# A transformer block on one core: all weights from float64 by two Prelu steps and one shift-or, the last additions on VectorE, the order computed anew

## The chip, the cores and the metric

The kernel runs on one core of a Trainium2 chip. The core's engines work side by side, each on a queue of its own: TensorE (PE; the loading of weights is shown apart, as PEld), VectorE (DVE), ScalarE (ACT), GpSimd (POOL) and SyncE (SP), which issues transfers. They wait for each other by semaphores. The metric is device microseconds of one execution. TensorE's clock has two levels, 1.2 and 2.4 GHz; the profile shows the granted clock as a share of the higher one.

## The reference

Softcapped attention, then a mixer over tokens and over channels, then the real part of a two-dimensional FFT with a normalisation and a second channel mixer. Batch 4, 12 heads, 448 tokens, 768 channels; cap is 30.

```python
scores = cap * np.tanh(scale * np.matmul(q, k.transpose(0, 1, 3, 2)) / cap)
attn = np.exp(scores - max); attn = attn / (sum + 1e-09)
x = attn @ v                                     # (4, 448, 768)
u = x + (np.maximum(x^T @ w_tok1, 0) @ w_tok2)^T   # 448 -> 256 -> 448
x = u + np.maximum(u @ w_ch1, 0) @ w_ch2           # 768 -> 1536 -> 768
u = x + np.real(fft2(x))
un = (u - mean) / np.sqrt(var + 1e-06)
out = u + np.maximum(un @ m_ch1, 0) @ m_ch2        # 768 -> 3072 -> 768
```

(Shortened: `max`, `sum`, `mean` and `var` are over the last axis.) The six weight matrices come as float64.

## The kernel before

**Storage.** Activations lie as 128 channels by 896 columns (two batches of 448 tokens): `z[bp][kc]`, bp 0 or 1 for the pair of batches, kc 0 to 5 for the block of channels; in traces `z_75` to `z_86`. Every product is made in three matmuls of rounded numbers (`mm3`, lines 248 to 250): a weight and an activation are each split into a high part and a low rest, and high·high, high·low and low·high are added up in PSUM. A weight of 128x768 with its parts is a *piece* (tiles `wh`, `wl`, four slots); PSUM has four slots `mm`, of 128 by two halves of 448.

**Weights from float64.** The chip's engines compute in float32, so a float64 weight is made from its two 32-bit words, or from bytes. There are two ways in the kernel before:
- `convert_v` (line 291), for the two pieces of each token-mixer matrix and the first two pieces of `c1`: ScalarE squares the high word, VectorE makes the bits with a shift-and (L313) and two and-or, shift-or steps (L317, L320), and a comparison and product (L323) clears tiny numbers.
- `convert` (line 331), for the other 70: the transfer (L351) lies three bytes off, so that the first word has the low bits of the exponent and the mantissa; three Relu steps on ScalarE (L276) make two powers of two out of the top byte, `cva` and `cvf`; on VectorE a shift-or (L359) makes the mantissa, an addition of integers (L279) joins the two powers, and one product (L368) makes the number.
- Then both split it: `wh` on ScalarE (L276), `wl` on VectorE or GpSimd (L279).

All elementwise sums of two tensors are recorded by one helper (L279) and all ScalarE copies by another (L276), so the tiles' names tell them apart.

**Order.** A planner (`Plan`) sorts all operations before they are emitted. It has for each a list of engines that it may take with an estimate of its time (`v`: VectorE; `a`: ScalarE; `t`: TensorE; `vp`: VectorE or GpSimd, whichever would end first), a rank from the order in which the program records it plus a shift by key (`SHIFT`), and constants (`fixed`) for what each instruction costs above its length. Each engine then runs its own list in that order; a change anywhere can move operations everywhere.

**Stages**, with their place in the profile: attention heads and token mixer (0 to about 290 us); first channel mixer (`group`, to about 700); the spectrum, `transform`, for either bp (560 to 840), which ends by adding its result `r` to `z`; the second mixer in 12 *Halves* for bp = 0 (to about 1100), in which a piece of m1 or m2 is converted, multiplied, and summed into `z`; for these `hidden` (L788, L792) makes the ReLU and its high and low parts (`r`), and `down` multiplies by the second weight and adds to `z`. Out of the converted m pieces, kept as `u` in float32, `combine` makes sums and differences of four (`u<-u`), which go to DRAM (`kept`). With them the second mixer of bp = 1 runs as Strassen products (1060 to the end). Their last sums, in `fold_in`, `fold_out`, `last15`, `last67` and `last23`, gather the products into the `z` of bp = 1, of two `z` tiles (`z<-z`) or of PSUM and `z` (`z<-mm,z`), and `store` writes them out (L1167).

## Time and profile before

| | |
|---|---|
| time, three runs | 1403.98, 1405.87, 1405.85 us (median 1405.85) |
| the profiled execution | 1406.29 us; its span 1404.40 us |
| TensorE busy | 1365.7 us, 97% of the span, 7470 instructions |
| VectorE busy | 1073.5 us, 76% |
| ScalarE busy | 704.1 us, 50% |
| GpSimd busy | 321.5 us, 23% |
| TensorE's granted clock, mean | 0.994 |
| the chain that ended last | PE 70%, DVE 15%, ACT 6%, DMA 5% |

The times agree within 0.2%. The page gives busy time by engine, the span in slices, and groups of instructions; the trace behind it gives the same for a stretch (from : to, in us from the span's start), the waits of one engine by the instruction that ended them, and single instructions in order of time. A busy TensorE is not TensorE at full clock: the granted clock stands beside it. An engine that idles costs nothing unless TensorE waits for it.

### The profile page before, as it was taken

How to read it: one execution, taken by the hardware profiler on the slowest of the kernel's cores; microseconds unless marked ns; L12 is line 12 of the kernel's file. 1: busy time of each engine (PE TensorE's matmuls, PEld its weight loads, DVE VectorE, ACT ScalarE, POOL GpSimd, SP SyncE). 2: the span in 40 equal slices, each digit the busy share in tenths (PEclk: the TensorE clock that was granted, in tenths of full speed). 3: DMA queues.
4: the chain of work that ended last, by engine and by line, in shares of the span. 5: the costliest groups of instructions: out<-in, count | busy, mean ns of one | idle time of the engine just before them, and what ended most of it. 6: DMA issues, size and time to landing. Idle time of an engine off the chain costs nothing.

```text
span 1404.4 us, 18761 instructions
## 1 busy us (share of the span) xinstructions
PE 1365.7 (97%) x7470; PEld 1135.0 (81%) x7470; DVE 1073.5 (76%) x1153; ACT 704.1 (50%) x824; POOL 321.5 (23%) x169
## 2 busy tenths in 40 slices
PE   8899999999999999999998999999999999999996
PEld 3344444599999999899998989988989998999996
DVE  7999988566776756557889699888977646667688
ACT  7878887576555544123233235444544553543432
POOL 4342433100000001000001122432314404414354
PEclk9999999999999999999999999999999999999999
DMA  4223221015666566512231168787868433344452
GB/s 125 86 73 105 83 73 47 7 68 157 247 201 194 193 222 207 160 46 91 90 136 57 46 223 298 272 309 259 301 229 298 152 113 100 103 124 133 130 178 99
DMA packets 67353, 211.90 MB, mean 151 GB/s; under 512 B 7552, under 2 KB 8960, under 8 KB 67266
## 3 DMA queue, kind: packets, MB, share of 16 engines
q1 hardware_dynamic: 66112, 208.08, 44.4%
q0 software_dynamic: 1152, 2.62, 0.7%
q8 instruction: 59, 0.97, 0.3%
q14 instruction: 28, 0.23, 0.0%
q10 hardware_dynamic: 2, 0.00, 0.0%
HBM read 145.30 MB, written 65.37 MB: 150 GB/s over the span
## 4 chain that ended last, share of the span: by engine, by line
PE 70%; DVE 15%; ACT 6%; DMA 5%; issue 2%; POOL 1%; SPq 0%; DVEq 0%; ACTq 0%; POOLq 0%
PE mm L249 20%; PE mm L248 20%; PE mm L250 20%; DVE t L279 3%; PE av L579 3%; DVE m L279 2%; DMA raw<-in_m_dram 2%; DMA wl<-kept 2%; PE sc L511 2%; DVE z L279 2%; ACT t L536 2%; ACT t L516 2%; PE av L595 2%; DVE u L279 2%; PE mx L706 1%
## 5 line engine op out<-in xcount | busy, mean ns | idle before, releaser
L249 PE MATMUL mm<-u,wh 128*128 128x448 f32 x798 | 293.7, 368 | 0.2 <-DVE u L279 0.2
L248 PE MATMUL mm<-u,wh 128*128 128x448 f32 x774 | 284.9, 368 | 4.9 <-DVE z L279 3.3
L250 PE MATMUL mm<-u,wl 128*128 128x448 f32 x774 | 284.6, 368 | 2.3 <-DMA wl<-kept 2.3
L279 DVE TENSOR_TENSOR z<-mm,z 128x896 f32<-128x896 f32 (+1 forms) x210 | 214.0, 1031 | 62.8 <-PE mm L250 61.4
L248 PE MATMUL mm<-r,wh 128*128 128x448 f32 x696 | 255.7, 367 | 0.7 <-DVE r L279 0.3
L249 PE MATMUL mm<-r,wh 128*128 128x448 f32 x678 | 249.4, 368 | 6.9 <-DVE r L279 6.6
L250 PE MATMUL mm<-r,wl 128*128 128x448 f32 x696 | 254.9, 366 | 0.0
L249 PEld LDWEIGHTS mm<-u,wh 128*128 128x128 f32 x798 | 151.1, 189 | 13.0 <-DVE u L279 0.6
L248 PEld LDWEIGHTS mm<-u,wh 128*128 128x128 f32 x774 | 146.5, 189 | 18.1 <-issue 3.7
L250 PEld LDWEIGHTS mm<-u,wl 128*128 128x128 f32 x774 | 146.5, 189 | 15.3 <-DMA wl<-kept 2.7
L276 ACT ACTIVATE cva<-raw 128x768 bf16<-128x768 int8 x70 | 63.4, 906 | 172.0 <-DVE u L368 66.4
L249 PEld LDWEIGHTS mm<-r,wh 128*128 128x128 f32 x678 | 127.8, 188 | 19.7 <-DVE r L279 8.7
L248 PEld LDWEIGHTS mm<-r,wh 128*128 128x128 f32 x696 | 131.2, 188 | 13.0 <-ACT r L276 0.8
L250 PEld LDWEIGHTS mm<-r,wl 128*128 128x128 f32 x696 | 131.2, 188 | 10.9
L528 POOL PARTITION_ALL_REDUCE mb<-m x48 | 93.6, 1997 | 166.9 <-DVE m L279 151.0
L276 ACT ACTIVATE r<-mm 128x896 fp32r<-128x896 f32 (+5 forms) x81 | 66.6, 826 | 119.2 <-PE mm L250 54.6
L279 DVE TENSOR_TENSOR t<-t,mb 112x1792 f32<-112x1792 f32 x48 | 107.3, 2254 | 5.5 <-POOL mb L528 5.4
L516 ACT ACTIVATE t<-sc,scl 112x896 f32<-112x896 f32 x96 | 92.4, 1004 | 12.4 <-PE sc L511 6.4
L276 ACT ACTIVATE wh<-wl 128x768 fp32r<-128x768 f32 x57 | 48.1, 845 | 95.3 <-DMA wl<-kept 93.8
L511 PE MATMUL sc<-qr 64*112 64x448 f32 x384 | 88.1, 569 | 7.7 <-ACT t L516 7.7
L536 ACT ACTIVATE t<-t,cap_sb 112x1792 f32<-112x1792 f32 x48 | 85.3, 1789 | 14.4 <-DVE t L279 14.1
L579 PE MATMUL av<-t,v 112*32 112x448 f32 x768 | 78.2, 542 | 2.0 <-ACT t L536 1.6
(205 smaller groups left out, 2238.1 us busy)
## 6 DMA issues: line engine op xcount, KB each, us to landing
raw<-in_m_dram SPq DMA_DIRECT2D x48, 767.6 KB, 5.1
wl<-kept SPq DMA_DIRECT2D x86, 384.0 KB, 3.5
kept<-u SPq DMA_DIRECT2D x60, 384.0 KB, 5.3
raw<-in_c_dram SPq DMA_DIRECT2D x22, 767.6 KB, 5.1
kept<-y SPq DMA_DIRECT2D x32, 384.0 KB, 5.7
wh<-kept SPq DMA_DIRECT2D x29, 384.0 KB, 3.1
raw<-kept SPq DMA_DIRECT2D x29, 384.0 KB, 3.1
qr<-in_qk_dram SPq DMA_DIRECT2D x23, 448.0 KB, 3.3
```

The lines of the kernel that those rows point to most:

```text
L248: T.matmul(out=dst, lhsT=wh, rhs=xh, start=first, stop=False, skip_group_check=more)
L249: T.matmul(out=dst, lhsT=wh, rhs=xl, start=False, stop=False, skip_group_check=more)
L250: T.matmul(out=dst, lhsT=wl, rhs=xh, start=False, stop=last, skip_group_check=more)
L276: pl.op(a(n), lambda e: A.activation(out=out(), in_=src(), func=func, **kw), reads, writes)
L279: pl.op(engs, lambda e: eng[e].tensor_tensor(out=out(), in0=in0(), in1=in1(), op=op), reads, writes)
L511: T.matmul(out=ps()[:CP, k, :S], lhsT=qr()[d, S + c * CP:S + (c + 1) * CP], rhs=qr()[d, :S], start=True, stop=True)
L516: pl.op(a(W2, 0.06), lambda e, c=c, ps=ps: A.activation(out=tl()[:, c], in_=ps()[:CP, :, :S], func=AF.Tanh, scale=scl[:CP, 0:1]), [ps, tl] ...
L528: pl.op({"P": 1.9}, lambda e, k=k: P.partition_all_reduce(mb()[:, k], mx()[:, k], CP, bass_isa.ReduceOp.max), [mx, mb], [kb], hold=0.75)
L536: pl.op(a(2 * W2, 0.1), lambda e, k=k: A.activation(out=tl()[:, :, k], in_=tl()[:, :, k], func=AF.Exp, scale=cap_sb[:CP, 0:1]), [tl], [ke])
L579: T.matmul(out=ps()[d, :S], lhsT=vv()[:, c, d], rhs=tl()[:, c, hd], start=(c == 0), stop=(c == NCH - 1))
L595: T.matmul(out=ps()[32 * k:32 * k + 32, :S], lhsT=ones[:CP, 0:32].bitcast(F32), rhs=tl()[:, c, hd], start=(c == 0), stop=(c == NCH - 1))
L706: T.matmul(out=ps()[:, :S], lhsT=channels_of(rt()[:, tb, c], kc % NJ), rhs=wt[:, tb, :], start=False, stop=last, skip_group_check=True)
```

## The change

1. `convert_v` is gone; all 76 conversions go by one way. `convert` now has a Relu and two Prelu steps on ScalarE, which make the bits of the number's sign and exponent as an integer (`field`, in `cvf`), and one operation on VectorE, a shift right by 5 of the first word and an or with `field`.
2. `piece` for the first two pieces of `c1` and `split_in` for the token mixer's split on VectorE.
3. The last sums (`fold_in`, `fold_out`, `last15`, `last67`) may only run on VectorE, and `last23` adds and stores its last tile by halves.
4. The Halves and the last visits of the first mixer are written as classes `First` and `Half` in place of `weights`, `ups` and `visit`; the points at which their operations are recorded are the same. `AHEAD`, the order in which weights are fetched ahead, has another order; the keys `hid` and `gather` have shift 0 (`gather` had −60); `fixed` takes its later values where the channel mixer starts, not after the token mixer's phase.
5. The planner's order is computed anew.

The instructions issued on TensorE keep their number (6681 matmuls); on VectorE there are 1020 in place of 1155, on ScalarE 839 in place of 827, on GpSimd 154 in place of 176, on SyncE 464 in both. There is one load of an activation table in each program.

```diff
-    def convert_v(src, rows, cols, h, l, writes, live=(), engs=v):
...
-        copy(cols, ff, lambda: word(1).bitcast(F32), [raw], [cv, cf], AF.Square)
-        pl.op({"V": 0.07 + cols / 1920}, lambda e: V.tensor_scalar(
-            out=ai(), in0=word(1), scalar1=3, scalar2=0x3FFFFFF8,
-            op0=ALU.logical_shift_left, op1=ALU.bitwise_and,
-        ), [raw, cv], [ca])
...
     def convert(src, rows, cols, x=None):
...
-        power(lambda: cat(0), top, 2048.0, (7 - 16 * 56) * 128, [raw], [cv, ca])
-        power(lambda: cat(1), top, -2048.0, 32768 - (7 + 16 * 72) * 128, [raw, cv], [cf])
-        power(lambda: cat(1), lambda: cat(1), -1.0, 32768, [cv], [cf])
-        pl.op({"V": 0.07 + cols / 1920}, lambda e: V.tensor_scalar(
-            out=word(), in0=word(), scalar1=5, scalar2=112 << 23,
-            op0=ALU.logical_shift_right, op1=ALU.bitwise_or,
-        ), [], [raw])
-        tt({"V": 0.07 + cols / 1920}, lambda: cat(0).bitcast(U16), lambda: cat(0), lambda: cat(1), ALU.add,
-           [cv, cf], [ca])
...
+        copy(cols, step, top, [raw], [cv, ca], AF.Relu, bias=72.0)
+        copy(cols, step, step, [cv], [ca], AF.Prelu, scale=-1.0, bias=16.0, alpha=KINK)
+        copy(cols, field, step, [cv, ca], [cf], AF.Prelu, scale=-FIELD / KINK, bias=-112.0 * FIELD, alpha=KINK)
         pl.op(v(cols), lambda e: V.scalar_tensor_tensor(
-            out=value(), in0=word().bitcast(F32), scalar=-256.0, in1=cat(0), op0=ALU.mult, op1=ALU.mult,
-        ), [raw, cv, ca], [x or raw])
+            out=value(I32), in0=word(), scalar=5, in1=field(), op0=ALU.logical_shift_right, op1=ALU.bitwise_or,
+        ), [raw, cv, cf], [x or raw])
...
             for i in range(2):
-                convert_v(tok1[i], CP, 2 * DTOK, lambda i=i: flat(w1h, i), lambda i=i: flat(w1l, i),
-                        (("w1h", i), ("w1l", i)))
+                value, key = convert(tok1[i], CP, 2 * DTOK)
+                split_in(2 * DTOK, value, key, lambda i=i: flat(w1h, i), lambda i=i: flat(w1l, i), "w1", i)
...
-        wu = [piece(c1[f], dve=True) for f in range(G)]
+        wu = [piece(c1[f], engs=v) for f in range(G)]
         split_u(0)
         split_u(1)
+        fixed.update(V=0.15, A=0.14, P=0.3)
...
-        AHEAD = [(n % 2, n // 2, n < 4 * SK2) for n in range(16)]
+        AHEAD = [(q, 4 * g + i, not g) for g in range(2) for q, i in
+                 ((0, 0), (0, 1), (0, 2), (0, 3), (1, 0), (1, 2), (1, 1), (1, 3))]
...
-                tt(vp(W2), lambda x=x: x, lambda x=x: x, lambda: a, ALU.add, ka, zk(1, k))
+                tt(v(W2), lambda x=x: x, lambda x=x: x, lambda: a, ALU.add, ka, zk(1, k))
...
         def last23(kc, ps):
-            gather(1, kc, 0, 2, ps, 0, False)
-            store(1, kc, kc == NJ - 1)
-
-        entered = []
+            end = kc == NJ - 1
+            for b in range(2) if end else (0,):
+                gather(1, kc, b, 1 if end else 2, ps, b, False)
+            store(1, kc, end)
```

**What moves.** Three places, each engine's own list before and after (lines of the changed kernel are other lines: L280 is its helper for sums, L323 the conversion's last step, L740 and L772 its `hidden` and `down`).

At the end of the spectrum (near 760 us), VectorE before: `r` is the spectrum's result, `z_83` and `z_86` are tiles that it is added to, `wl` is a weight's low part, and the last row is the sum for which the next matmul waits.

```order
L279 TENSOR_TENSOR r_6318<-r_6318,mm_6259 128x450 x2
L827 TENSOR_TENSOR mm_6291<-mm_6291,y_5870 128x2x448
L279 TENSOR_TENSOR z_83<-r_6318,z_83 128x2x225
L279 TENSOR_TENSOR wl_6310<-wl_6310,wh_6309 128x768
L279 TENSOR_TENSOR z_83<-r_6318,z_83 128x2x223
L279 TENSOR_TENSOR z_86<-r_6318,z_86 128x2x225
L279 TENSOR_TENSOR z_86<-r_6318,z_86 128x2x223
L279 TENSOR_TENSOR z_80<-mm_6291,z_80 128x896
```

And now:

```order
L280 TENSOR_TENSOR r_6231<-r_6231,mm_6174 128x450 x2
L772 TENSOR_TENSOR mm_6206<-mm_6206,y_5788 128x2x448
L280 TENSOR_TENSOR z_83<-r_6231,z_83 128x2x225
L280 TENSOR_TENSOR z_83<-r_6231,z_83 128x2x223
L280 TENSOR_TENSOR z_86<-r_6231,z_86 128x2x225
L280 TENSOR_TENSOR z_86<-r_6231,z_86 128x2x223
L280 TENSOR_TENSOR z_80<-mm_6206,z_80 128x896
```

The subtraction that makes `wl` has left VectorE's list between the sums of `r`; it stands on GpSimd ahead of three additions `r<-r,u`, which are three of the four that stood there.

In the Half stage (near 1030 us), VectorE before: `raw`, `cva` and `u` are the conversion of a piece, `mm` times `y` and the `r` subtraction make the operand of the next matmuls.

```order
L279 TENSOR_TENSOR r_8457<-mm_8353,r_8447 128x896
L279 TENSOR_TENSOR cva_8430<-cva_8430,cvf_8431 128x768
L368 SCALAR_TENSOR_TENSOR u_8466<-raw_8391,cva_8430 128x768
L359 TENSOR_SCALAR raw_8433<-raw_8433 128x768
L792 SCALAR_TENSOR_TENSOR mm_8435<-mm_8435,y_5870 128x2x448
L279 TENSOR_TENSOR wl_8502<-u_8466,wh_8501 128x768
L279 TENSOR_TENSOR cva_8474<-cva_8474,cvf_8475 128x768
L368 SCALAR_TENSOR_TENSOR u_8529<-raw_8433,cva_8474 128x768
L279 TENSOR_TENSOR r_8531<-mm_8435,r_8512 128x896
```

And now:

```order
L740 SCALAR_TENSOR_TENSOR mm_8226<-mm_8226,y_5788 128x2x448
L323 SCALAR_TENSOR_TENSOR u_8293<-raw_8222,cvf_8273 128x768
L280 TENSOR_TENSOR r_8309<-mm_8226,r_8301 128x896
L280 TENSOR_TENSOR z_78<-mm_8285,z_78 128x896
L323 SCALAR_TENSOR_TENSOR u_8335<-raw_8279,cvf_8319 128x768
L740 SCALAR_TENSOR_TENSOR mm_8305<-mm_8305,y_5788 128x2x448
L280 TENSOR_TENSOR wl_8369<-u_8293,wh_8368 128x768
L280 TENSOR_TENSOR r_8391<-mm_8305,r_8381 128x896
```

Shift-or and addition are gone from between; one step of conversion for each piece remains in front of the `r` subtraction.

In the same stage, GpSimd before, where `u<-u` are the sums of `combine`:

```order
L279 TENSOR_TENSOR wl_8490<-u_8425,wh_8489 128x768
L279 TENSOR_TENSOR u_8529<-u_8466,u_8529 128x768
L279 TENSOR_TENSOR u_8654<-u_8654 128x448
L279 TENSOR_TENSOR u_8666<-u_8666 128x448
L279 TENSOR_TENSOR wl_8737<-u_8652,wh_8736 128x768
L279 TENSOR_TENSOR u_8652<-u_8425,u_8652 128x768
L279 TENSOR_TENSOR u_8425<-u_8425,u_8380 128x768
L279 TENSOR_TENSOR u_8380<-u_8652,u_8380 128x768
L279 TENSOR_TENSOR u_8592<-u_8592,u_8380 128x768
```

And now, at the stage's start:

```order
L280 TENSOR_TENSOR wl_6892<-u_6817,wh_6891 128x768
L280 TENSOR_TENSOR u_6858<-u_6817,u_6858 128x768
L280 TENSOR_TENSOR u_6817<-u_6703,u_6817 128x768
L280 TENSOR_TENSOR u_6703<-u_6858,u_6703 128x768
L280 TENSOR_TENSOR u_6746<-u_6746,u_6703 128x768
L280 TENSOR_TENSOR u_6911<-u_6897,u_6911 128x768
L280 TENSOR_TENSOR u_7153<-u_7151,u_7153 128x768
L280 TENSOR_TENSOR u_7151<-u_7151,u_7178 128x768
L280 TENSOR_TENSOR u_7178<-u_7153,u_7178 128x768
L280 TENSOR_TENSOR u_7149<-u_6889,u_7149 128x768
L280 TENSOR_TENSOR u_6889<-u_6889,u_6780 128x768
```

The sums come in runs of three or four with `wl` subtractions between them before, and in a run of ten now.

At the very end, VectorE before: sums of two `z` tiles stand between those that take a product out of PSUM.

```order
L279 TENSOR_TENSOR z_84<-z_84,z_78 128x896
L279 TENSOR_TENSOR z_84<-mm_11208,z_84 128x448
L279 TENSOR_TENSOR z_81<-mm_11231,z_81 128x896
L279 TENSOR_TENSOR z_82<-mm_11239,z_82 128x896
L279 TENSOR_TENSOR z_83<-z_83,z_80 128x448
L279 TENSOR_TENSOR z_85<-mm_11208,z_85 128x448
L279 TENSOR_TENSOR z_83<-mm_11267,z_83 128x896
L279 TENSOR_TENSOR z_86<-mm_11223,z_86 128x448
```

And now:

```order
L280 TENSOR_TENSOR z_80<-mm_11045,z_80 128x448
L280 TENSOR_TENSOR z_83<-z_83,z_80 128x448
L280 TENSOR_TENSOR z_86<-z_86,z_80 128x896
L280 TENSOR_TENSOR z_84<-mm_11063,z_84 128x448
L280 TENSOR_TENSOR z_85<-mm_11063,z_85 128x448
L280 TENSOR_TENSOR z_86<-mm_11079,z_86 128x448
L280 TENSOR_TENSOR z_81<-mm_11087,z_81 128x896
L280 TENSOR_TENSOR z_82<-mm_11105,z_82 128x896
L280 TENSOR_TENSOR z_83<-mm_11123,z_83 128x448 x2
```

The sums of two `z` tiles that GpSimd had in the last 70 us are on VectorE and come first; the last six take products out of PSUM, and the last of these is made by halves.

## Rows read from the trace of the kernel before

**Rows 1.** The page's part 1, busy time and share; and one row of the groups.
```profile
PE 1365.7 (97%) x7470; PEld 1135.0 (81%) x7470; DVE 1073.5 (76%) x1153; ACT 704.1 (50%) x824; POOL 321.5 (23%) x169
...
L1710 ACT ACT_TABLE_LOAD x1 | 1.3, 1283 | 1.3 <-PEq L1836 1.3
```

**Rows 2.** Stretch of the heads: length; busy PE, PEld, DVE, ACT, POOL; clock; DMA.
```profile
20.00:160.00 140.00, 132.27 (x986) 61.12 (x983) 136.06 (x131) 114.67 (x121) 51.09 (x26) 1.00 0.27 83
```

**Rows 3.** Groups by line, the six `convert_v`: count, busy us, mean ns, idle before.
```profile
L313 DVE TENSOR_SCALAR cva<-raw 112x512 int32<-112x512 int32 (+2 forms) x6 | 3.5, 584 | 0.0
...
L317 DVE SCALAR_TENSOR_TENSOR cva<-raw,cva 112x512 int32<-112x512 int32 (+2 forms) x6 | 5.8, 961 | 0.1
...
L320 DVE SCALAR_TENSOR_TENSOR cva<-raw,cva 112x512 int32<-112x512 int32 (+2 forms) x6 | 5.8, 959 | 0.1
...
L323 DVE SCALAR_TENSOR_TENSOR cvf<-cvf,cva 112x512 f32<-112x512 f32 (+2 forms) x6 | 4.5, 746 | 0.0
```

**Rows 4.** Groups by line, `convert`'s 70: steps on ScalarE, addition and shift-or.
```profile
L276 ACT ACTIVATE cva<-raw 128x768 bf16<-128x768 int8 x70 | 63.4, 906 | 172.0 <-DVE u L368 66.4 <-DMA raw<-in_m_dram 33.8 <-DMA raw<-in_c_dram 32.3
...
L276 ACT ACTIVATE cvf<-cvf 128x768 bf16<-128x768 bf16 x70 | 59.1, 845 | 1.9
...
L279 DVE TENSOR_TENSOR cva<-cva,cvf 128x768 uint16<-128x768 bf16 x70 | 43.7, 624 | 41.1 <-ACT cvf L276 40.9
...
L359 DVE TENSOR_SCALAR raw<-raw 128x768 int32<-128x768 int32 x70 | 43.4, 620 | 10.9 <-DMA raw<-in_c_dram 7.2 <-DMA raw<-in_m_dram 3.7
```

**Rows 5.** TensorE's waits: for whom, us in total, times, longest.
```profile
PE sc L511 <- ACT t L516: 7.7, 16, 1.7
...
PE mm L249 <- DVE r L279: 6.6, 6, 1.8
...
PE mm L248 <- DVE z L279: 6.4, 3, 3.3
...
PE mm L250 <- DMA wl<-kept: 2.3, 1, 2.3
```

**Rows 6.** Four more stretches, columns as in rows 2.
```profile
760.00:780.00 20.00, 16.66 (x71) 14.89 (x70) 15.64 (x15) 3.85 (x5) 5.91 (x3) 0.83 0.07 20
...
820.00:1050.00 230.00, 224.64 (x1086) 204.50 (x1085) 203.63 (x218) 115.30 (x140) 65.27 (x34) 0.99 0.78 274
...
1180.00:1360.00 180.00, 180.00 (x885) 165.91 (x884) 120.31 (x113) 73.23 (x85) 63.02 (x30) 1.00 0.41 129
...
1380.00:1400.00 20.00, 13.65 (x65) 11.50 (x63) 19.00 (x18) 0.54 (x1) 8.42 (x4) 1.00 0.24 93
```

**Rows 7.** Timeline of VectorE near 1036 us: start, length, operation.
```profile
1033.33 1.97 DVE L279 TENSOR_TENSOR wl<-u,wh 128x768 fp32r<-128x768 f32 x1 [1.78 <-ACT wh L276]
...
1035.80 0.96 DVE L368 SCALAR_TENSOR_TENSOR u<-raw,cva 128x768 f32<-128x768 f32 x1
...
1038.68 0.95 DVE L279 TENSOR_TENSOR wl<-u,wh 128x768 fp32r<-128x768 f32 x1
```

**Rows 8.** Timeline near 760 us: two of VectorE, one of GpSimd.
```profile
761.82 2.87 DVE L279 TENSOR_TENSOR wl<-wl,wh 128x768 fp32r<-128x768 f32 x1
...
766.22 4.07 DVE L279 TENSOR_TENSOR z<-mm,z 128x896 f32<-128x896 f32 x4
...
757.08 6.79 POOL L279 TENSOR_TENSOR r<-r,u 128x896 f32<-128x896 f32 x3 [195.75 <-ACT r L276]
```

**Rows 9.** Timeline of the end: three of VectorE, two of GpSimd.
```profile
1378.82 3.01 DVE L279 TENSOR_TENSOR z<-z 128x896 f32<-128x896 f32 x1
...
1384.36 5.01 DVE L279 TENSOR_TENSOR z<-z 128x896 f32<-128x896 f32 x3
...
1398.22 1.62 DVE L279 TENSOR_TENSOR z<-mm,z 128x896 f32<-128x896 f32 x2 [0.74 <-PE mm L250]
...
1385.51 2.90 POOL L279 TENSOR_TENSOR z<-z 128x896 f32<-128x896 f32 x1 [2.67 <-DVE z L279]
...
1389.44 2.76 POOL L279 TENSOR_TENSOR z<-z 128x896 f32<-128x896 f32 x1 [1.03 <-DVE z L279]
```

More of the change, by code (lines that the diff above doesn't have):

```diff
@@ L342, in top, with step, field, value @@
             return raw().bitcast(I8)[:rows, :cols, 4]
-        def cat(i):
-            return cv()[i][:rows, :cols]
-        def power(out, src, scale, bias, reads, writes):
-            copy(cols, out, src, reads, writes, AF.Relu, scale=scale, bias=float(bias))
+        def step():
+            return cv()[0][:rows, :cols]
+        def field():
+            return cv()[1].bitcast(I32)[:rows, :cols]
+        def value(dt=F32):
+            return (x().bitcast(dt) if x else raw().rearrange("p a b -> p (a b)").bitcast(dt))[:rows, :cols]
         pl.op(
```

297 lines of the change are left out of this document (140 added, 157 removed).

## The prediction

> **What bounds the kernel now.** I read the busy times first, then the stretches, then what TensorE waited for, then the rows around its longest stops. TensorE is busy for 1365.7 of 1404.4 us [rows 1], and the change leaves its 6681 matmuls as they are. So nearly the whole time is TensorE's own work, and a change on the other engines can win only what TensorE stands still or runs at less than its full 2.4 GHz: some 39 us of idle time plus a little clock. Where these lie decides. In the heads (20 to 160 us) TensorE idles 7.7 of 140 us while VectorE is busy for 136.06 and ScalarE for 114.67 [rows 2]: there VectorE paces by its sum. From 1180 to 1360 us TensorE does not idle at all, and VectorE works two thirds of the time [rows 6]; whatever the change takes from VectorE there is worth nothing. The rest of what can be won is a handful of stops. The waits name their owners: ScalarE's softcap step in the heads (7.7 us in 16 stops), VectorE's `r` subtraction (6.6 us in 6 stops, the Half stage), VectorE's `z` addition (6.4 us in 3, the spectrum's end and the kernel's end) and one weight fetch (2.3 us) [rows 5].
>
> **Part 1, the six early conversions** (token mixer, and the first two channel pieces). Removed on VectorE: the four steps of `convert_v`, 3.5 + 5.8 + 5.8 + 4.5 = 19.6 us [rows 3]; added: one step of the same six widths, for which I take the dearest-placed of the four, the last, at 4.5. VectorE −15.1 us. On ScalarE one Square becomes three steps: 12 steps more, at no more than the 0.845 us of a 768-wide one [rows 4], so at most +10.1 us. Prelu itself stands in no row; I price it as the Relu steps that it replaces. What is it worth? At most the 7.7 us that TensorE idles in the heads, at least nothing, since ScalarE becomes the busier one where the stops are already named after it. ScalarE 114.67 + 10.1 stays well under 140, though, and VectorE falls clear of its 97%. I take a third: **−2.6 us** (0 to −7.7).
>
> **Part 2, the other 70 conversions.** The uint16 addition (43.7 us) and the shift-or (43.4 us) go, the last step stays as one operation, and ScalarE keeps three steps [rows 4]: VectorE −87.1 us. All of it lies beside TensorE; only stops count. Between 820 and 1050 us TensorE is busy 224.64 of 230 us, at 0.99 of its clock [rows 6], so 5.4 us idle and about 2.3 us of clock (0.01 × 230) can come back, 7.7 in all. The stop at 1036 us shows how it arises: `wl` takes 1.97 us on VectorE, then come the addition, 0.62 in the mean [rows 4], and the conversion's last step, 0.96 [rows 7], and only then the `r` subtraction for which TensorE waits. In the new order the addition and the shift-or are gone from in front of it, and the conversion's last step remains. The two removed steps are 0.62 to 1.24 us (one or both of them in front) of a stop of 1.8 us at the longest [rows 5], half of it or a little more. I take **−4.2 us** (0 to −7.7). The fetch stop of 2.3 us, where transfers meet, may shrink by the 0.62 us of the step that the chain to the next piece loses [rows 4, 5]: **−0.6 us** (0 to −2.3).
>
> **Part 3, the spectrum's end.** From 760 to 780 us TensorE idles 3.34 us and its granted clock is 0.83 in the mean, so another 0.17 × 20 = 3.4 us go to the clock behind the stop [rows 6]. VectorE has `wl` of 2.87 us, slowed beside GpSimd's run of three additions (6.79 us), just ahead of the `z` additions that free PSUM [rows 8]. In the new order this `wl` stands on GpSimd, ahead of its three additions, and VectorE's `z` additions come 2.87 us earlier: that leaves 0.5 us of the stop, and I give back half of the clock, 1.7: **−4.6 us** (0 to −6.7).
>
> **Part 4, the end.** From 1380 to 1400 us TensorE is busy 13.65 us and VectorE 19.00 [rows 6]; 1.8 us of the 6.35 idle lie behind the last matmul, which VectorE's last additions follow at 1398.2 [rows 9], so 4.55 can be won. VectorE's additions of two SBUF tiles cost 3.01 for one and 5.01 for three there [rows 9], 2.0 us each, while the same shape out of PSUM takes 4.07/4 = 1.02 [rows 8]; GpSimd works at such additions at the same time. With GpSimd's moved to VectorE this contention is gone: four cost 4.1 in place of 8.02, −3.9 us; the two additions that GpSimd starts here [rows 9] add 2.0, up to 4.1 if the four instructions that the stretch counts on it [rows 6] all come at this time. Net between 0 and −4.55 (the whole idle time, as the earlier ones now find VectorE free); I take **−3.0 us**. VectorE's last two additions, one of 896 and one of 448 columns, took 1.62 us behind the last matmul [rows 9]. In the new order the last addition is made by halves, each behind its own matmuls, and nothing stands behind it, so only a half's 0.6 us (the longer one's 1.02 cut in two, and a start) remain there: **−1.0 us** (0 to −1.0).
>
> **Part 5, what moves for no purpose.** The order of every engine is new. Stretches without a stop may get one: TensorE's longest wait of an ordinary kind is 1.8 us [rows 5]. One such, less what chance closes elsewhere: **+1.5 us** (0 to +6). The earlier change of the planner's constants, the new order of fetches ahead, and the conversion for the first channel pieces move operations, and add no transfer.
>
> **Sum.** −2.6 − 4.2 − 0.6 − 4.6 − 3.0 − 1.0 + 1.5 = −14.5 us. The profiled execution is 1406.29 us (its span 1404.40), 0.4 us above the median; the saving is taken off the median: 1405.85 − 14.5 = **1391.3 us**. Its own range goes from 1383 (the bounds of parts 2 to 4, except the last 1.0: −7.7 − 2.3 − 6.7 − 4.55, with the rest as taken, is −23.4) to 1398 (half the gain).
>
> **Rivals.**
> - *The contention stays* (parts 3 and 4 give nothing): VectorE's queue at both ends fills with the additions that GpSimd had, or GpSimd's new place for `wl` slows it as much as before. −14.5 + 7.6 = −6.9: 1399 us. For it: two engines' work on one. Against: 2.0 us against 1.02 for the same sum of columns.
> - *GpSimd's long runs hold up VectorE in the Half stage.* In the new order GpSimd's additions for the Strassen weights, runs of three or four before, stand in runs of up to ten between the same `wl`s. While GpSimd worked at a `wl` of its own, a `wl` on VectorE took 1.97; five microseconds later 0.95 [rows 7]: 1 us more at seven places is +7, and part 2 falls to 0. −14.5 + 4.2 + 7 = −3.3: 1402.5 us. By the Trainium skill, "SBUF — State Buffer", "Who interferes with whom", a VectorE instruction with two SBUF inputs contends with a GpSimd instruction that reads SBUF, and the later one blocks for all of the other; the row of 1.97 against 0.95 agrees with this, and by that rule the new conversion step (raw words and field both in SBUF) is as exposed as the old one was.
> - *Everything goes*: all bounds at once, −30: 1376 us. Against: some stop always remains, since the slots of PSUM are few.
> - *Only the order counts*: the new order opens as many stops as the lighter engines close; part 5 is +15, and the time is about 1406 us, no change.
> - *Slower: Prelu is dear.* Were a Prelu step twice a Relu step, 2 × 0.845, each conversion would take 1.7 us longer on ScalarE. In the Half stage ScalarE (115.30 of 230 us busy) has room for the sum, but its `r` copies for TensorE stand behind these steps: 1.7 us at each of nine such stops is +15 in place of −4.2, and the heads lose 6 in place of −2.6. −14.5 + 19.2 + 8.6 = +13.3: 1419 us. It decides from the point where the extra eats the 14.5: 27.8 us of swing for 0.845, so from a Prelu of about 1.29 us. The rows show no Prelu; the Relu steps, from int8 with a stride or from bf16, take 0.906 and 0.845 [rows 4], near the same whatever the operands, which speaks against a double price and leaves it a few hundredths. By the Trainium skill, "ScalarE activation tables: per-element evaluation and per-set limits", "What a function is on this engine", an activation costs the same whichever table is read. No run shows it for Prelu yet; by that rule this rival has no ground and the time is the forecast's.
> - *The table is loaded anew* at each change between Prelu and the softcap's functions: the one load of the trace takes 1.283 us [rows 1]; 76 conversions with two changes each would be 195 us of ScalarE. The changed program has one load as before, so this could only be if that one did not serve them all: over 100 us slower, with next to no chance.
>
> **Chances.** Forecast 0.58; contention stays 0.12; long runs 0.10; only the order 0.07; everything 0.06; dear Prelu 0.06; table 0.01. A measurement of this kernel tells 0.2% (2.8 us) from no change. Faster by more than that: 0.58 + 0.12 + 0.06 and 0.06 of the long runs, less 0.02 for the forecast's own tail: 0.80. Within it: 0.03 of the long runs, 0.04 of the order, 0.02: 0.09. Slower: the rest, 0.11. The range from 1380 to 1405 holds the forecast nearly whole, the first two rivals, and a part of the others.
>
> **What would show it.** In the profile of the changed kernel: one ScalarE row of Prelu per conversion step near 0.85 us and one table load; VectorE busy about 1073.5 − 15 − 87 plus some 20 for the 22 operations that GpSimd loses, so near 990; GpSimd without any `z` row in the last 70 us, and VectorE's `z<-z` near 1.0 us there; no stop of 3 us and no clock of 0.83 near 760 us; fewer `r` stops between 820 and 1050. I would be wrong if TensorE's busy time, not its idle time, moved; if new stops of over 2 us stand in the stretches that had none; or if Prelu took over 1.2 us.

## The result, and the profile of the changed kernel

The changed kernel takes 1389.01 us (median of 4 runs, 1388.1 to 1389.77) against 1405.54: a ratio of 0.9884, 95% interval 0.9867 to 0.9901. Run once more beside others it took 1389.27 us against 1406.8 on that chip, 0.9874 (0.9851 to 0.9897). The forecast was 1391.3.

The page of the changed kernel, busy times and the shares of the chain that ended last; they answer to [rows 1]:

```profile
PE 1363.5 (98%) x7470; PEld 1133.8 (82%) x7470; DVE 983.0 (71%) x1018; ACT 714.0 (51%) x836; POOL 264.3 (19%) x147
...
PE 87%; DVE 7%; ACT 4%; DMA 2%; issue 0%; DVEq 0%; ACTq 0%
```

TensorE's busy time fell by 2.2 us and the span by 17.1, from 1404.4 to 1387.3: 14.9 us of the gain are TensorE's idle time. VectorE lost 90.5 us, GpSimd 57.2; of the chain that ended last VectorE holds 7% in place of 15%.

TensorE's waits, which answer to [rows 5] (for whom, us in total, times, longest):

```profile
PE sc L468 <- ACT t L473: 6.9, 11, 2.2
PE mm L250 <- DVE r L280: 2.4, 2, 1.8
PE mm L251 <- DMA wl<-kept: 2.4, 1, 2.4
PE mm L249 <- DVE z L280: 1.2, 2, 0.9
PE mm L249 <- ACT z L277: 1.1, 1, 1.1
```

The `r` waits fell from 6.6 us in 6 stops (five in the Half stage; one of 1.64 us at 1384 us, which the prediction also put there) to 2.4 in 2 (0.66 in the Half stage, and a new one of 1.77 at 1351 us), the `z` waits from 6.4 to 1.2. The fetch stop took 2.4 us here, and less in a second profile of the same kernel (run changed_again, below):

```profile
PE mm L251 <- DMA wl<-kept: 1.7, 1, 1.7
```

Stretches, as in [rows 2, 6] and at the same work, since all runs up to 17 us earlier at the end (length; busy PE, PEld, DVE, ACT, POOL; clock; DMA share; GB/s):

```profile
1363.00:1383.00 20.00, 17.64 (x84) 15.03 (x82) 19.24 (x23) 2.39 (x5) 2.37 (x1) 1.00 0.21 83
...
750.00:770.00 20.00, 19.12 (x95) 17.38 (x95) 19.44 (x21) 5.46 (x8) 4.74 (x3) 1.00 0.18 59
803.00:1040.00 237.00, 235.59 (x1151) 215.52 (x1150) 173.96 (x168) 119.56 (x146) 72.82 (x38) 1.00 0.78 284
20.00:160.00 140.00, 135.81 (x1014) 59.81 (x1016) 129.86 (x117) 125.09 (x134) 51.08 (x27) 0.98 0.29 89
1160.00:1340.00 180.00, 180.00 (x886) 165.87 (x885) 118.39 (x120) 71.13 (x83) 41.65 (x22) 1.00 0.42 130
```

In the heads VectorE fell from 136.06 to 129.86 of 140 us and ScalarE rose from 114.67 to 125.09; TensorE idles 4.2 us there in place of 7.7. The Half stage has VectorE at 174 of 237 us where it had 204 of 230, and TensorE idle for 1.4 us in place of 5.4. At the end VectorE is as full as it was, 19.24 of 20 us.

The conversion's steps, by operation (count, busy us, mean ns), which answer to [rows 4]:

```profile
L277 ACT ACTIVATE cvf<-cva 128x768 int32<-128x768 bf16 x72 | 60.8, 844 | 4.0 <-DVE y L323 2.3
L277 ACT ACTIVATE cva<-cva 128x768 bf16<-128x768 bf16 x72 | 60.5, 840 | 1.7
...
L323 DVE SCALAR_TENSOR_TENSOR u<-raw,cvf 128x768 int32<-128x768 int32 x32 | 35.6, 1113 | 23.2 <-ACT cvf L277 23.2
...
L323 DVE SCALAR_TENSOR_TENSOR y<-raw,cvf 128x768 int32<-128x768 int32 x16 | 15.3, 956 | 21.7 <-ACT cvf L277 19.7 <-DMA kept<-y 1.0 <-DVE z L280 1.0
```

A Prelu step of 128x768 takes 0.840 us, and 0.844 where it writes integers; the Relu step that it replaced took 0.845. The one step left on VectorE takes what the old product took, 0.96 to 1.13.

**Where the time went.** TensorE issues the same 7470 instructions in every kernel here. The time from the start of one to the start of another, by their number, therefore compares stages between kernels. I cut at numbers 2000 (end of the token mixer), 4250, 4500 (around the spectrum's end), 6000 (end of the Half stage), 7250 and 7469 (the last). In us, from one profile each:

| kernel | heads | first mixer | spectrum's end | Half | Strassen | end |
|---|---|---|---|---|---|---|
| before | 288.9 | 436.4 | 51.4 | 312.9 | 256.8 | 50.4 |
| changed | 286.0 | 435.8 | 45.9 | 306.6 | 254.6 | 51.1 |
| changed_again | 286.1 | 433.6 | 46.4 | 306.4 | 255.0 | 49.6 |
| *before, with one thing changed* | | | | | | |
| wl_to_gpsimd | 289.5 | 436.9 | 50.9 | 311.7 | 256.5 | 52.0 |
| no_squares | 289.5 | 435.9 | 45.4 | 314.1 | 256.1 | 50.4 |
| last_sums_alone | 289.8 | 434.8 | 50.5 | 311.2 | 256.6 | 48.4 |
| early_alone | 284.1 | 436.1 | 50.3 | 312.0 | 256.6 | 50.4 |
| late_alone | 290.0 | 435.5 | 50.3 | 308.0 | 256.2 | 52.4 |
| *changed, with one thing undone or added* | | | | | | |
| old_steps_planned | 285.6 | 436.4 | 46.2 | 314.8 | 254.3 | 51.0 |
| old_sums | 286.0 | 435.3 | 46.2 | 306.3 | 254.6 | 58.7 |
| later_sums | 285.6 | 434.1 | 46.2 | 311.4 | 255.2 | 50.6 |
| pad_early | 303.2 | 435.6 | 46.1 | 306.6 | 254.6 | 49.6 |
| pad_vector | 286.1 | 439.1 | 46.2 | 317.0 | 254.9 | 51.1 |
| pad_scalar | 288.5 | 443.9 | 46.2 | 312.8 | 254.6 | 49.6 |

From before to changed: −2.9, −0.6, −5.5, −6.3, −2.2, +0.7, together −16.8; behind the last matmul 6.2 us became 5.9.

A single profile is good to some 2 us in a stage, and to 5 in the Half stage (below). The changed kernel's own two profiles, with the same instructions in the same order, differ by 2.2 us in the first mixer and by 1.5 at the end, and the granted clock has a part in it. From 565 to 575 us, around the fetch stop, it was 0.83 in the one and 1.00 in the other; at the end, around a stop of 1.77 us that both have, 0.74 from 1350 to 1355 us in the one and 1.00 from 1349 to 1354 in the other. At the spectrum's end the profile before is the longest of the four that have the old order's stop unaltered (50.3 to 51.4 us, with last_sums_alone, early_alone and late_alone); five of the changed order have 45.9 to 46.4, so that the gain there is 4.5 us in the mean and 5.5 in the pair.

### The profile page after: what moved, and what is told of

Same layout as the page of the kernel before. It is cut to its first block, busy times and chain, and to the rows that moved or that the text cites. A ratio compares the mean times of both kernels' runs of the same rounds, so it can differ in the third digit from the quotient of the medians.

```text
span 1387.3 us, 18639 instructions
## 1 busy us (share of the span) xinstructions
PE 1363.5 (98%) x7470; PEld 1133.8 (82%) x7470; DVE 983.0 (71%) x1018; ACT 714.0 (51%) x836; POOL 264.3 (19%) x147
## 4 chain that ended last, share of the span: by engine, by line
PE 87%; DVE 7%; ACT 4%; DMA 2%; issue 0%; DVEq 0%; ACTq 0%
PE mm L249 23%; PE mm L251 23%; PE mm L250 23%; PE av L536 5%; PE sc L468 4%; PE av L552 2%; DVE z L280 2%; PE mx L663 2%; ACT t L473 2%; DMA wl<-kept 1%; ACT t L493 1%; DVE u L280 1%; DVE r L280 1%; PE av L563 1%; DVE t L280 1%; PE mx L249 1%
## 5 line engine op out<-in xcount | busy, mean ns | idle before, releaser
L251 PE MATMUL mm<-u,wl 128*128 128x448 f32 x786 | 288.5, 367 | 2.8 <-DMA wl<-kept 2.4
L280 DVE TENSOR_TENSOR z<-mm,z 128x896 f32<-128x896 f32 (+1 forms) x211 | 213.7, 1027 | 70.5 <-PE mm L251 69.5
L249 PE MATMUL mm<-r,wh 128*128 128x448 f32 x696 | 254.9, 366 | 0.5 <-issue 0.5
L277 ACT ACTIVATE r<-mm 128x896 fp32r<-128x896 f32 (+5 forms) x87 | 71.9, 830 | 117.6 <-PE mm L251 60.7
L277 ACT ACTIVATE cva<-raw 128x768 bf16<-128x768 int8 (+2 forms) x76 | 67.4, 887 | 111.3 <-DMA raw<-in_m_dram 74.6
L485 POOL PARTITION_ALL_REDUCE mb<-m x48 | 90.2, 1927 | 166.2 <-DVE m L280 152.8
L280 DVE TENSOR_TENSOR t<-t,mb 112x1792 f32<-112x1792 f32 x48 | 109.1, 2302 | 5.4 <-POOL mb L485 5.3
L280 POOL TENSOR_TENSOR wl<-wl,wh 128x768 fp32r<-128x768 f32 x17 | 32.5, 1915 | 335.4 <-ACT wh L277 327.1
```

The source lines that it names most:

```text
L249: T.matmul(out=dst, lhsT=wh, rhs=xh, start=first, stop=False, skip_group_check=more)
L251: T.matmul(out=dst, lhsT=wl, rhs=xh, start=False, stop=last, skip_group_check=more)
L277: pl.op(a(n), lambda e: A.activation(out=out(), in_=src(), func=func, **kw), reads, writes)
L280: pl.op(engs, lambda e: eng[e].tensor_tensor(out=out(), in0=in0(), in1=in1(), op=op), reads, writes)
L485: pl.op({"P": 1.9}, lambda e, k=k: P.partition_all_reduce(mb()[:, k], mx()[:, k], CP, bass_isa.ReduceOp.max), [mx, mb], [kb], hold=0.75)
```

## The experiments

**The spectrum's end: is it the subtraction?** VectorE's first sum of the spectrum and the other three in the kernel before, with the `wl` of [rows 8] between them:

```profile
759.77 2.12 DVE L279 TENSOR_TENSOR z<-r,z 128x450 f32<-128x450 f32 x1
...
764.61 1.68 DVE L279 TENSOR_TENSOR z<-r,z 128x446 f32<-128x446 f32 x3
```

In the kernel before, that `wl` is given to GpSimd, and nothing else moves.

```diff
...
-        halves(DM, lambda: x().bitcast(F32), part(w, 0), x, [w, ws[2]], ws[1:], engs)
+        copy(DM, part(w, 0), lambda: x().bitcast(F32), [w, ws[2]], [ws[1]])
+        on = eng["P"] if len(fetched) == 1 else None
+        fetched.append(k)
+        pl.op(engs(DM), lambda e: (on or eng[e]).tensor_tensor(
+            out=x(), in0=x().bitcast(F32), in1=part(w, 0)().bitcast(F32), op=ALU.subtract
+        ), [w, ws[2], ws[1]], [ws[2]])
```

> The kernel before with one operation moved: the subtraction that makes wl_6310, 2.87 us on VectorE at 761.8 us between the sums of the spectrum's end, runs on GpSimd between its additions r<-r,u. Nothing else moves. My step (part 3): VectorE's z additions come 2.87 us earlier, the stop of 3.34 us near 767 us falls to about 0.5 and the granted clock behind it stays up: 4 to 5 us less, some 1401 us. Rival (the stop is the r additions' or the fetch's, not this subtraction's): the stop stays over 2 us and the time within 1 us of 1405.5. A second rival: GpSimd's wl, now late behind an addition of 2.3 us, makes TensorE wait for wl itself, 1 to 2 us.

Measured: 1406.67 us, ratio 1.0 (0.9987 to 1.0014). VectorE there (start, length, operation):

```profile
760.81 5.76 DVE L279 TENSOR_TENSOR z<-r,z 128x450 f32<-128x450 f32 x4
766.49 4.07 DVE L279 TENSOR_TENSOR z<-mm,z 128x896 f32<-128x896 f32 x4
```

and TensorE's stop:

```profile
767.72 0.71 PE L248 MATMUL mm<-u,wh 128*128 128x448 f32 x1 [2.57 <-DVE z L279]
```

The subtraction is gone from VectorE, and the four sums `z<-r,z` now take 5.76 us where they took 2.12 and 1.68. The `z` additions start 5.7 us after the first of these sums, before it was 6.45 [rows 8], and the stop is 2.57 us in place of 3.34. My step fell. Whether the subtraction was slowed like its neighbours or slowed them, this run alone does not tell, since on GpSimd it stands beside the same sums; the next run does.

**The spectrum's end: is it GpSimd's additions?** In the kernel before, the additions of squares that the planner gave to GpSimd are left out.

```diff
-                    tt(vp(W2), lambda: pair(m.var), lambda: pair(m.var), lambda: pair(sq), ALU.add, [sq], [m.var])
+                    pl.op(vp(W2), lambda e: e == "V" and V.tensor_tensor(
+                        out=pair(m.var), in0=pair(m.var), in1=pair(sq), op=ALU.add), [sq], [m.var])
```

> The kernel before without the additions of squares r<-r,u that GpSimd makes near 757 us (the variance of half of the batches is then a part of itself; nothing else is left out). If GpSimd's additions are what holds up VectorE's sums of the spectrum there: the four z<-r,z take 0.6 to 0.7 us each in place of 3.8 us together, wl 0.95 in place of 2.87, the z additions come 3 us earlier, and the stop of 3.34 us falls under 0.6 with its clock, 4 to 5.5 us between 755 and 772 us. Rival (the stop comes from the products or from the fetch): 2.5 us or more of it stay.

Measured: 6.0 us less at the spectrum's end (51.4 to 45.4; 4.9 to 5.1 against the three other profiles with that stop), 1400.3 us in one run beside 1404.85. VectorE at the same place:

```profile
759.69 0.62 DVE L279 TENSOR_TENSOR z<-r,z 128x450 f32<-128x450 f32 x1
760.22 0.96 DVE L279 TENSOR_TENSOR wl<-wl,wh 128x768 fp32r<-128x768 f32 x1
761.10 1.69 DVE L279 TENSOR_TENSOR z<-r,z 128x446 f32<-128x446 f32 x3
762.70 4.08 DVE L279 TENSOR_TENSOR z<-mm,z 128x896 f32<-128x896 f32 x4
```

`wl` takes 0.96 in place of 2.87, the first sum 0.62 in place of 2.12, and the `z` additions start at 762.70 in place of 766.22; the stop of 3.34 us is gone. So it was GpSimd's run of three additions of 2.3 us each, against VectorE's operations on two SBUF tiles; the subtraction was a bystander. In the changed kernel two of these additions stand there, the third on VectorE later. Two `wl` are made before they begin: the earlier fetch's on GpSimd, the later one's, which in the kernel before stood between the sums, on VectorE.

```profile
748.36 1.85 POOL L280 TENSOR_TENSOR wl<-wl,wh 128x768 fp32r<-128x768 f32 x1 [190.56 <-ACT wh L277]
...
750.42 0.96 DVE L280 TENSOR_TENSOR wl<-wl,wh 128x768 fp32r<-128x768 f32 x1 [0.61 <-ACT wh L277]
```

The sums still take 4.22 us:

```profile
755.49 4.22 DVE L280 TENSOR_TENSOR z<-r,z 128x450 f32<-128x450 f32 x4
759.63 3.07 DVE L280 TENSOR_TENSOR z<-mm,z 128x896 f32<-128x896 f32 x3
```

GpSimd at that time:

```profile
753.55 4.60 POOL L280 TENSOR_TENSOR r<-r,u 128x896 f32<-128x896 f32 x2 [3.34 <-ACT r L277]
```

From the first sum to the `z` additions it is 4.1 us in place of 6.45. Which does more, the earlier `wl` or the addition that GpSimd lost, was not tried apart; the first run shows that `wl` put among GpSimd's additions gains next to nothing.

**The heads: are they VectorE's?** The changed kernel with the VectorE time of part 1 put back, as idle operations in its place.

```diff
...
+        def join(e):
+            for _ in range(4 if early else 0):
+                V.tensor_scalar(out=word(), in0=word(), scalar1=0, scalar2=0,
+                                op0=ALU.logical_shift_right, op1=ALU.bitwise_or)
...
```

> The changed kernel, same order, with four idle VectorE operations (shifts by nothing, 0.58 us in the mean) put in front of the last step of the six early conversions, about 14 us: the VectorE time that part 1 took out is back. If the heads' gain (2.9 us up to 289 us) comes from VectorE, 2 to 4 us come back there. Rival (the heads are set by the softcap's chain through ScalarE): under 0.7 us.

Measured: the idle operations took 16.6 us, and the heads 303.2 us in place of 286.0, +17.2; 1404.83 us in one run. TensorE's longest groups of waits:

```profile
PE sc L478 <- ACT t L483: 8.6, 11, 2.5
PE av L573 <- DVE rs L581: 6.8, 4, 3.2
```

Waits for VectorE's `rs` (the softmax's sums) are new. In this order VectorE paces the heads, though it was busy for 129.86 of 140 us there and not to the full: work that the order has not provided for costs what it lasts. The other side, the new conversion for these six alone in the kernel before, with the order computed for it:

```diff
...
-                convert_v(tok1[i], CP, 2 * DTOK, lambda i=i: flat(w1h, i), lambda i=i: flat(w1l, i),
-                        (("w1h", i), ("w1l", i)))
+                value, key = convert_n(tok1[i], CP, 2 * DTOK)
+                split_in(2 * DTOK, value, key, lambda i=i: flat(w1h, i), lambda i=i: flat(w1l, i), "w1", i)
...
```

> The kernel before with the new conversion for the six early matrices alone (15.1 us less on VectorE, some 10 more on ScalarE), the order computed for it. By part 1 of the prediction 2.6 us less up to 289 us. After two runs I doubt it: the changed kernel with the old steps, planned, ran its heads in 285.6 us, as fast as with the new ones (286.0), so the 2.9 us there may be the order's. Then the heads here take 288 to 290 us, as in the kernel before (288.9 to 289.8), and the time stays within 1.5 us of before.

Measured: 1400.0 us, ratio 0.9955 (0.9939 to 0.9971), the heads 284.1 us against 288.9 to 290.0 in five profiles of the old order: −5.4 from their mean. My doubt fell, and part 1's direction held. The stretch of [rows 2]:

```profile
20.00:160.00 140.00, 136.00 (x1030) 60.15 (x1028) 129.26 (x117) 120.82 (x129) 50.70 (x27) 0.98 0.28 87
```

**The Half stage: is it VectorE's queue?** The changed kernel with two idle operations put in front of each later conversion's last step.

```diff
...
+            if late:
+                V.tensor_scalar(out=word(), in0=word(), scalar1=0, scalar2=0,
+                                op0=ALU.logical_shift_right, op1=ALU.bitwise_or)
+                V.tensor_tensor(out=step().bitcast(U16), in0=step().bitcast(U16), in1=step().bitcast(U16),
+                                op=ALU.bitwise_or)
...
```

> The changed kernel, same order, with two idle VectorE operations put in front of the last step of each of the 70 later conversions (a shift by nothing of the words, 0.62 us, and an or of the powers with themselves, 0.62 us): the VectorE time that the change took out, about 87 us, is back, and nothing else is. If the gain of the second mixer's first stage (6.3 us between 777 and 1090 us of before) comes from VectorE's queue being shorter, 4 to 7 us come back, to 1393 to 1396 us, as stops of 0.5 to 2 us behind r subtractions between 800 and 1040 us. Rival (the new order did it): within 1.5 us of 1389.0.

Measured: 1406.42 us, 0.9995 (0.9978 to 1.0012): 17 us, the whole gain, is lost; in the profiled run 14.7, of them 10.4 us in the Half stage and 3.3 in the first mixer. Waits in the Half stage:

```profile
PE mm L250 <- DVE r L280: 3.2, 5, 1.0
PE mm L249 <- DVE z L280: 2.0, 2, 1.5
PE mm L249 <- ACT wh L277: 1.8, 2, 1.3
```

The place was right in the main and the size was not: VectorE time that the order has not provided for cost more than the change had won there (old_steps_planned, below, has the same steps provided for). The new conversion for the 70 later pieces alone, in the kernel before, with the order computed for it:

```diff
...
-        power(lambda: cat(0), top, 2048.0, (7 - 16 * 56) * 128, [raw], [cv, ca])
...
+        copy(cols, step, step, [cv], [ca], AF.Prelu, scale=-1.0, bias=16.0, alpha=KINK)
+        copy(cols, field, step, [cv, ca], [cf], AF.Prelu, scale=-FIELD / KINK, bias=-112.0 * FIELD, alpha=KINK)
...
```

> The kernel before with the new conversion for the 70 later pieces alone (87 us less on VectorE), the order computed for it. By part 2: 4.2 us less, nearly all in the Half stage, which took 311.2 to 314.1 us in four profiles of that order and 306.6 twice and 311.4 in three of the changed order. The spectrum's end keeps its stop if GpSimd's additions of squares still stand together there (51 us from 725 to 777; 46 without the stop). If the conversion were the whole gain: 16 us.

Measured: 1400.1 us, 0.995 (0.9931 to 0.9968). The Half stage took 308.0 us against 311.2 to 314.1 in five profiles of the old order (early_alone's among them), −4.4 from their mean (312.4), and the end of the spectrum kept its stop. Waits from 777 to 1092 us:

```profile
PE mm L251 <- DVE r L281: 1.7, 2, 1.0
```

And the changed kernel with both old conversions back, the order computed for them:

```diff
...
+        if engs is v:
+            convert_v(src, 128, DM, part(w, 0), part(w, 1), ws[1:], [w])
+            return w, ws
...
```

(and `convert` and the token mixer's two calls as before.)

> The changed kernel with both old conversions, and the order computed for them: new classes, new constants, last sums on VectorE, fetch order stay. Put behind the changed order without the planner knowing, the same VectorE work cost 14 us. If the planner can hide a good part of it, 1393 to 1399 us: the gain splits about evenly between the conversion and the rest. If the conversion is the whole gain: 1403 us or more. If the order is: under 1391 us.

Measured: 1395.06 us, 0.9922 (0.9897 to 0.9948). The Half stage is 8.3 us longer than in the changed kernel; all other stages are within 1 us or so of it, the heads too. About 6 of the 16 us are then the conversion's in the new order, and the rest belongs to all else that changed: last sums, constants, order of fetches, and the order itself, which this run does not tell apart. Alone in the kernel before, each with an order of its own, the two groups of conversions gave 6.8 and 6.7 us by the medians (1406.8 to 1400.0 and 1400.1): conversion and order in part win the same microseconds.

**ScalarE's price.** One more step in each conversion:

```diff
...
+            A.activation(out=step(), in_=top(), func=AF.Relu, bias=72.0)
+            A.activation(out=step(), in_=step(), func=AF.Relu)
...
```

> The changed kernel, same order, with one more ScalarE step (a Relu of what is already positive, 0.845 us) in each of the 76 conversions, 64 us of ScalarE. The prediction's rival of a dear Prelu put 27.8 us on twice this, so about 14 us for this: 1403 us, by stops at the r copies of the Half stage and in the heads. Rival: ScalarE, busy for 51% of the span, takes it in the gaps and the conversions run ahead of need: 0 to 4 us, most of it in the heads, 1389 to 1393 us.

Measured: 1403.55 us, 0.9975 (0.9961 to 0.999), +14.5 to the changed kernel: the price that the rival put on it. But by the profile 8.1 us of it lie in the first mixer, of which the rival did not speak, 6.2 in the Half stage, 2.5 in the heads; the sum came out by luck. The longest wait is

```profile
PE mm L249 <- DVE r L740: 5.3, 2, 4.0
```

in the first mixer; its longer stop, 3.98 us, ends at 410.72 us. VectorE's `r` is only the last link there: it needs the copy `r<-mm` that ScalarE makes of the same product. On ScalarE that copy comes at 408.64, behind the steps of a conversion that itself waited 2.01 us for its words, in a `raw` tile that the conversion before it gives back later than the order had provided for:

```profile
405.35 0.90 ACT L321 ACTIVATE cva<-raw 128x768 bf16<-128x768 int8 x1 [2.01 <-DMA raw<-in_c_dram]
...
408.64 0.90 ACT L277 ACTIVATE r<-mm 128x896 fp32r<-128x896 f32 x1
```

**The end.** The last sums on VectorE alone and the last tile's by halves, in the kernel before:

```diff
...
-                tt(vp(W2), lambda x=x: x, lambda x=x: x, lambda: a, ALU.add, ka, zk(1, k))
+                tt(v(W2), lambda x=x: x, lambda x=x: x, lambda: a, ALU.add, ka, zk(1, k))
...
```

> The kernel before with the last sums alone on VectorE and the last tile's sum by halves; everything up to about 1330 us is in the old order. By parts 4 and the tail of the prediction: 4.0 us less, 1401.5 us, with VectorE's z<-z near 1.0 us. Rival, from the trace of the changed kernel, where the last 58 us give only 0.7 us: the sums that GpSimd had now stand in VectorE's list in front of the operands of the next products, and the gain is within 1.5 us of nothing. In both the end from the last matmul on is about 0.5 us shorter.

Measured: 1404.55 us, 0.9992 (0.9975 to 1.0009). TensorE was done 2.0 us earlier (50.4 to 48.4), and VectorE was not: its last operations start up to 4.9 us after the last matmul's start at 1392.30.

```profile
1396.10 1.08 DVE L279 TENSOR_TENSOR z<-z 128x896 f32<-128x896 f32 x1
1397.21 0.62 DVE L279 TENSOR_TENSOR z<-mm,z 128x448 f32<-128x448 f32 x1
```

Behind the last matmul stand 9.0 us in place of 6.2. The other way round, the changed kernel with the old last sums, the last tile's whole:

```diff
...
-                tt(v(W2), lambda x=x: x, lambda x=x: x, lambda: a, ALU.add, ka, zk(1, k))
+                tt(vp(W2), lambda x=x: x, lambda x=x: x, lambda: a, ALU.add, ka, zk(1, k))
...
```

> The changed kernel with the last sums as before: VectorE or GpSimd, the last tile's sum whole. The last 58 us took 50.4 us from one matmul to the last in the kernel before, 51.1 and 49.6 in profiles of the changed order, 48.4 where the last sums alone were changed. By the prediction's part 4 it would lose 4.0 us. By these profiles it loses 0 to 2 us, with VectorE's z<-z near 1.6 us again and about half a microsecond more behind the last matmul.

Measured: 1394.26 us, 0.9912 (0.9886 to 0.9939), 5.0 us over the changed kernel beside it; the end took 58.7 us. TensorE's waits from 1335 us on:

```profile
PE mm L250 <- DVE r L280: 3.6, 1, 3.6
PE mm L249 <- DVE z L280: 2.5, 1, 2.5
```

GpSimd and VectorE ahead of the first of them:

```profile
1341.04 8.02 POOL L280 TENSOR_TENSOR z<-z 128x896 f32<-128x896 f32 x3
1349.02 2.64 POOL L280 TENSOR_TENSOR raw<-raw 128x768 fp32r<-128x768 f32 x1
```

```profile
1347.09 2.92 DVE L1467 SCALAR_TENSOR_TENSOR y<-y,r 128x896 f32<-128x896 f32 x1
1349.93 2.68 DVE L280 TENSOR_TENSOR r<-r,u 128x896 fp32r<-128x896 f32 x1
```

A run of three sums and a subtraction on GpSimd holds up two of VectorE's operations, 2.92 and 2.68 us in place of 1.09, that make the last products' operand. So part 4 is worth nothing clear of noise in the old order and 5 us by the median in the new one (by profiles 7.6 to 9.1 us of the end, less 1.2 that stand fewer behind the last matmul): the same edit, priced by what stands beside it.

What is still lost at the end of the changed kernel stands in VectorE's list:

```profile
1341.85 1.08 DVE L280 TENSOR_TENSOR z<-z 128x896 f32<-128x896 f32 x1
1342.84 2.73 DVE L280 TENSOR_TENSOR r<-r 128x896 fp32r<-128x896 f32 x1
1345.50 1.08 DVE L280 TENSOR_TENSOR z<-z 128x896 f32<-128x896 f32 x1
...
1350.15 1.09 DVE L280 TENSOR_TENSOR r<-r,u 128x896 fp32r<-128x896 f32 x1
```

beside one subtraction that GpSimd kept:

```profile
1342.46 2.17 POOL L280 TENSOR_TENSOR raw<-raw 128x768 fp32r<-128x768 f32 x1 [2.00 <-ACT raw L277]
```

and TensorE behind it:

```profile
1351.29 0.47 PE L250 MATMUL mm<-r,wh 128*128 128x448 f32 x1 [1.77 <-DVE r L280]
...
1354.26 0.57 PE L251 MATMUL mm<-u,wl 128*128 128x448 f32 x1
```

Two wide sums, `z_84` and `z_85`, go ahead of the subtraction at 1350.15, and between them an `r<-r` takes 2.73 us beside GpSimd, where another of its shape takes 1.09 at 1363.05; TensorE stops 1.77 us, and some matmuls behind it take 0.57 us in place of 0.37 (the granted clock was 0.74 from 1350 to 1355 us). The wide sums of `fold_out` held back:

```diff
+            tt(v(W2), lambda: zh, lambda: zh, lambda: a[:, 1:2, :].to_broadcast([128, 2, S]), ALU.add,
+               [*ka[1:], behind], zk(1, NJ + kc))
...
+                    fold_out(kc, cur.r["1"][1])
```

> The changed kernel with the three wide sums of fold_out (z_84, z_85, z_86, 1.08 us each) held behind the subtraction that makes the last products' operand. In the changed kernel two of them stand in VectorE's list ahead of it, at 1341.9 and 1345.5 us, and TensorE then stops 1.77 us at 1351 us and runs ten matmuls at a lowered clock. If the moved sums are what eats the gain of part 4: the stop at 1351 us is gone or under 0.5 us with its clock, 3 to 4 us, less what the sums cost later where VectorE is full; 1386 to 1388 us. Rival (the chain of Strassen operands is late by itself): the stop stays over 1 us, and the time is 1389 or more.

Measured: 1390.36 us, 0.9897 (0.9864 to 0.9929), no better. Two of its waits:

```profile
PE mm L249 <- DVE u L1454: 2.2, 1, 2.2
PE mm L249 <- ACT wh L277: 2.1, 1, 2.1
```

The stop at 1351 is gone and another of 2.2 us came 13 us later, behind the sums that were held back. The end is 50.6 us, as before the edit (51.1 and 49.6). VectorE is busy there for 19 of 20 us, and this other order did not help.

**The changed kernel as it is**, once more, for its Half stage:

> The changed kernel once more, on the same chip as the three others and beside the kernel before: 1387 to 1391 us, and a further profile of the Half stage, which took 306.6 us in two profiles of this order and 311.4 in one with the same instructions up to there. If that stage varies from run to run by some 5 us, the gain there is 4 us in the mean, as part 2 has it, and not the 6.3 us that the first two profiles show.

Measured: 1389.27 us. Four profiles of the changed order have a Half stage of 306.3 to 306.6 us, a fifth (later_sums) has 311.4, with a stop of 2.05 us behind ScalarE's `wh` at 831.6 us that these four don't have. Its instruction lists are the changed kernel's up to 1340 us, so it is the execution that differed. ScalarE had stood there for the words of a weight, three operations ahead of that `wh`:

```profile
828.49 0.89 ACT L277 ACTIVATE cva<-raw 128x768 bf16<-128x768 int8 x1 [3.04 <-DMA raw<-in_m_dram]
```

At the same operation the first profile of the changed kernel shows a wait of 0.68 us. pad_scalar has a stop at the same matmul, of 2.44 us at 844.9. Why these words came later against the rest in that one profile is open. The gain of that stage is then 5.9 us (312.4 to 306.5), with such outliers apart.

## Why the prediction was right, point by point

The time came 2.3 us below the forecast, inside its own range. The direction and the rough size followed from one reading, that only TensorE's idle time could be won and that a handful of stops held it; the terms were not all right, and that the sum came so close is in part luck.

- **Part 1, −2.6 us**: −2.9 in the changed kernel, −5.4 alone. Right, and right in its reason as far as pad_early shows it: VectorE time put in costs what it lasts. But the old steps, planned in the new order, ran the heads as fast (285.6), with VectorE busy for 134.61 of 140 us in the stretch of [rows 2], so VectorE's sum alone does not set the length, and the order is a second way to the same 3 us. The two don't add up; that ScalarE's softcap waits, which remain (6.9 us, as 7.7 before), are the reason was not tried.
- **Part 2, −4.2 us**: −4.4 alone, −5.9 with the new order, which with the old steps gave the stage nothing (314.8 us). Right. Which operations stood in front was read from one stop; pad_vector brings back stops of that kind (3.2 us for `r`), and others, for `z` and `wh`, of up to 1.5 us.
- **The fetch, −0.6 us**: not shown. The stop went from 2.3 us to 2.4 in one profile of the changed kernel and to 1.7 in the other; over all runs it is 2.0 to 2.4 us with the order of the kernel before or near it and 1.7 to 2.5 with the new one.
- **Part 3, −4.6 us**: −5.5 in the pair of profiles, −4.5 in the mean, but by another cause. The step that failed is "this `wl` stands on GpSimd": it was an earlier fetch's `wl` that went there, and the one in question moved up on VectorE. And moved by itself it gave half a microsecond. The prediction named the slowing, and still took all 2.87 us as won when the subtraction goes: 2.87 us for an operation that takes 0.95 elsewhere was the sign of GpSimd's additions, not a cost of its own. By the Trainium skill, "SBUF — State Buffer", "Who interferes with whom", a VectorE instruction with two SBUF inputs and a GpSimd instruction that reads SBUF exclude each other; no_squares agrees with it (0.96 against 2.87, 0.62 against 2.12).
- **Part 4, −3.0 us, and the tail, −1.0**: mis-sized. The end gave +0.7 and −0.8 in two profiles, the tail −0.3. VectorE stayed as full as it was (19.24 of 20 us), for the sums that GpSimd had came at full length, and the order put two of them ahead of an operand. This is the rival "the contention stays" in the form that it names first, VectorE's queue in place of the contention; and some contention stayed too, in the `r<-r` of 2.73 us.
- **Part 5, +1.5 us**: new stops came at the end, one of 1.77 us and one of 1.07 behind ScalarE's `z`, and are in the end's figure. Not foreseen: the stop of 1.6 us at 1179 us went, which in [rows 6] lies a microsecond outside the stretch that I took for free of stops; ScalarE had waited there 3.67 us for GpSimd's `r<-r`, the last of three operations of 2.1 to 2.7 us that follow each other. The Strassen stage gained 2.2 us.
- **The rivals.** Dear Prelu: fell, at 0.84 us; by the Trainium skill, "ScalarE activation tables: per-element evaluation and per-set limits", "What a function is on this engine", the table read makes no difference to the cost, and the rows agree. Its price held in the sum, not in the places: +14 forecast for half of it, +14.5 measured, the most of it in the first mixer. Long runs of GpSimd in the Half stage: the longest there is of five sums, 10.86 us from 845.61, not of ten, since GpSimd waits for transfers in between (19.03 us before the next five). They slow VectorE no more than before: the conversion's last step into `u` takes 1.11 us in the mean, before it was 1.13, and the stage ran in 306.5 us. Only the order: between the two, since the order and the conversion each hold a part.

In the pair of profiles part 3 was 1 us too small, part 2 two, the Strassen stage's 2.2 us were not seen, and from the end, tail and new stops some 3 us more were expected than came: errors that offset each other in the sum.
